# A run-time overflow test on the sums of exponentials, with a branch to a general path

## The chip, the core and the metric

The kernel runs on one core of one Trainium2 chip. The core has five engines with their own instruction streams: PE (matrix multiply into PSUM), DVE (vector), ACT (activation functions), POOL (general vector work) and SP (which here only issues transfers). They meet through semaphores. The time is device microseconds of one execution. The three timed runs of the kernel before took 146.16, 146.58 and 146.92 us, median 146.58. A separate execution was profiled; all views below are of it.

## The reference

One token block x of 2048 tokens by 512 channels goes through two branches, and a per-token gate mixes them:

```
qkv = x @ wqkv; q, k, v in 32 heads of 16
pq = q @ w_phi[h]; pk = k @ w_phi[h]
phi_q = concat(softmax(pq), softmax(-pq)); phi_k = concat(softmax(pk), softmax(-pk))
kv = sum_s phi_k[s] v[s]; z = sum_s phi_k[s]
a = ((phi_q @ kv) / (phi_q @ z + 1e-6)) @ wo
b = relu(x @ w1) @ w2
g = sigmoid((x * gate_w).sum(-1))
out = g * a + (1 - g) * b
```

All inputs and the output are bf16. The attention is linear: kv and z are sums over all tokens, so no query can be finished before the last key is in. The softmax runs over the 16 features of one head.

## The kernel before, in words

The tokens are cut into NT = 16 tiles of 128. The work is written down by hand as one list of operations per engine (`_Plan.op`, `_Plan.dma`); each entry names the events that it waits for, and `emit` (L45) turns the list of an engine into instructions, in exactly that order, with one counting semaphore per producer. An engine's list is therefore its queue: an operation waits behind everything in front of it.

Before the tile loop the kernel loads x, transposes it, computes the first chunk of h = relu(x @ w1) (`slab`, L549, `hunit`, L261) and folds w_phi into wqkv (`pre`, L303). Because a softmax does not change when a constant is taken off all its inputs, only 15 features per head are multiplied, each already reduced by feature 16; the 16th exponential is a constant 1 written once into EB (L579). No maximum is subtracted.

The attention stage handles one tile per step. `atile(m)` (L322) multiplies x by the folded weights into two PSUM banks, ACT takes exp of the plus and minus form into the buffer `EB[:, b]` (b = m mod 5; slots 0 and 1 for q, 2 and 3 for k). `kchain` (L383) sums the 16 features on DVE into the right half of `ZB[:, b]` (L392), takes the reciprocal (L394) and scales on POOL (L396). `qchain` (L402) sums q's features into the left half of ZB (L405), takes a reciprocal (L410), and POOL scales one half (L412, L414); SP then issues a DMA transpose to PHQ (L419). `kv(m)` (L439) adds phi_k transposed times v into banks 6 and 7, three tiles behind. Between these, PE is filled with pieces of h for later chunks (`mid`, L598). The last two tiles are done in halves.

After the last kv, `kvfin` (L454) moves kv and z to SBUF, and the final stage begins. `nd(m)` (L476) multiplies phi_q by kv and z on PE into banks 0 and 1 (even m) or 2 and 3 (odd m), DVE takes a reciprocal (`rd`, L486) and a product (`om`, L490) into one of three buffers OTM, and SP issues a transpose into OT (`to`, L496). `finB(m)` (L501) is h @ w2, 11 matmuls; `finA(m)` (L511) is OT @ wo, 4 matmuls, and ACT scales it by the gate (`ta`, L518). `comb(m)` (L523) adds both on DVE (`cb`, L527) into one of three buffers OSB and issues the output transfer (`out`, L532). `gate()` (L469) makes g and 1-g from exp. OTM and OSB lie in WQK, whose weights are no longer needed by then. The last tile's output is cut into 384 and 128 columns; the first part is sent by SP, the second by ACT, and SP waits for the `fin` semaphore (L674).

The order at the start of the final stage is nd(0), the last qchain, gate, finB(0), nd(1), finB(1), nd(2), nd(3), finA(0).

Of the kernel before, what the change touches and what calls it, by code (L numbers as in the profile page):

```python
# [5 lines left out]
ACT = mybir.ActivationFunctionType  # L6
ALU = mybir.AluOpType
# [6 lines left out]
class _Plan:  # L14


    def __init__(self, engines):
        self.ops = {e: [] for e in engines}
        self.count = {}
        self.events = {}  # L20
        self.first = {}

    def early(self, eng):
        self.first[eng] = len(self.ops[eng])

    def op(self, eng, fn, after=(), ev=None):
        if ev is not None:
            self.count[eng] = self.count.get(eng, 0) + 1
            self._set(ev, eng, self.count[eng])
        self.ops[eng].append((fn, tuple(after), eng if ev is not None else None, 1))  # L30
# [11 lines left out]
        assert ev not in self.events, ev  # L42
        self.events[ev] = (sem, value)

    def emit(self, name, eng, sems, block):  # L45
        seen = {}
        start = len(block)
        gate = next(i for i, ins in enumerate(block)
                    if ins.engine == eng.engine and ins.concise_opcode() == "EventSemaphore") if name in self.first else 0
        for k, (fn, after, sem, inc) in enumerate(self.ops[name]):  # L50
            if k == self.first.get(name):
                new = block[start:]
                del block[start:]
                block[gate:gate] = new
            need = {}
            for ev in after:
                s, v = self.events[ev]
                need[s] = max(need.get(s, 0), v)
            for s, v in need.items():
                if seen.get(s, 0) < v:  # L60
                    seen[s] = v
                    eng.wait_ge(sems[s], v)
            if fn is not None:
                ins = fn(eng)
                if sem is not None:
                    ins.then_inc(sems[sem], inc)


def bass_gated_mix__linear_kernel_hedgehog__dense_activation_relu__prompt_kernel(
# [17 lines left out]
    P = 128  # L87
# [13 lines left out]
    LAG = 3  # L101
    KU = KT - 1
    NR = DFF - KU * P

    with ExitStack() as es:
        E = es.enter_context
# [31 lines left out]
        OMG = E(nc.sbuf_tensor("OMG", [P, NT], FP32))  # L138
        RDEN = E(nc.sbuf_tensor("RDEN", [P, 2, H], FP32))
        TFA = E(nc.sbuf_tensor("TFA", [P, 2, D], BF16))  # L140
        PS = E(nc.psum_tensor("PS", [P, 8, 512], FP32))

        XS = OT[:, 0, :].rearrange("p (j d) -> p j d", j=4)
        WQKT = PHQ[:, :, S - 512:S]
        OTM = WQK[:, 0, 0:3 * D].rearrange("p (a b) -> p a b", a=3)
        OSB = WQK[:, 1, 0:3 * D].rearrange("p (a b) -> p a b", a=3)
        EPS = 8 * 512
        EBS = NB * 4 * 2 * D
        ones = bass.AP(tensor=ONE, offset=0, ap=[[1, P], [0, 512]])
# [172 lines left out]
        def atile(m, b0=0):  # L322
            b = m % NB
            first = xready(m // 4)
            order = [(dt, w) for dt in range(NDT) for w in range(2)]
            if m - 1 in split:
                order = [(dt, w) for w in (1, 0) for dt in range(NDT)]
            if m == 0:
                order = [(dt, w) for w in (0, 1) for dt in range(NDT)]
            for i, (dt, which) in enumerate(order):  # L330
                p.op("pe", lambda e, dt=dt, which=which: e.matmul(  # L331
                    PS[:, b0 + which, 0:DE], XT[:, dt, m * P:(m + 1) * P], WQK[:, which, dt * DE:(dt + 1) * DE],
                    start=(dt == 0), stop=(dt == NDT - 1)),
                    after=(first if i == 0 else []) + (free[b0 + which] if dt == 0 else [])
                    + ([f"pc{4 * which + dt}"] if m == 0 else []),
                    ev=(f"qk{m}" if i == 7 else None))
            src = PS[:, b0:b0 + 2, 0:DE].rearrange("p a (h f) -> p a h f", h=H)
            base = b * 8 * D
            busy = [f"tq{m - NB}", f"pk{m - NB}", f"pq{m - NB}"] if m >= NB else []

            def expo(s, w, ev):
                step = (4 * D, 2 * D)[s]
                off = base + s * (2 * D + 16)
                scale = (1.0, -1.0)[s]
                if w is None:
                    dst = bass.AP(tensor=EB, offset=off, ap=[[EBS, P], [step, 2], [32, H], [1, FE]])
                    s_ = src
                else:
                    dst = bass.AP(tensor=EB, offset=off + w * step, ap=[[EBS, P], [32, H], [1, FE]])
                    s_ = src[:, w, :, :]  # L350
                p.op("act", lambda e: e.activation(dst, s_, ACT.Exp, scale=scale),  # L351
                     after=[f"qk{m}"] + busy, ev=ev)
# [12 lines left out]
            qchain(m)  # L365

        def half(m, w, bank):
            b = m % NB
# [33 lines left out]
        def qchain(m):  # L402
# [17 lines left out]
                out=PHQ[:, :, m * P:(m + 1) * P], in_=EB[:, b, 0, :]),  # L420
                f"tq{b}", after=[f"pq{m}", f"cst{b}"] + (["pm7"] if m == 12 else []), ev=f"tq{m}")

        def vtile(m, eng="act", bank=2):
            b = m % VB
            for dt in range(NDT):
                p.op("pe", lambda e, dt=dt: e.matmul(  # L426
                    PS[:, bank, :], XT[:, dt, m * P:(m + 1) * P], WV[:, dt, :],
                    start=(dt == 0), stop=(dt == NDT - 1)),
                    after=((xready(m // 4) + ["wv"] + free[bank]) if dt == 0 else ()),
                    ev=(f"v{m}" if dt == NDT - 1 else None))  # L430
            dst, src = VS[:, b, :, 0:64], PS[:, bank, :].rearrange("p (g c) -> p g c", g=NG)
# [7 lines left out]
        def kv(m):  # L439
            b = m % NB  # L440
            vb = m % VB
            for g in range(NG):
                after = []
                if g == 0:
                    after = [f"pk{m}", f"cv{m}", f"one{vb}"]
                    if m == 0:
                        after += free[6] + free[7]
                p.op("pe", lambda e, g=g: e.matmul(  # L448
                    PS[:, 6 + g // 4, (g % 4) * GW:(g % 4) * GW + 65],
                    EB[:, b, 3, g * P:(g + 1) * P], VS[:, vb, g, 0:65],  # L450
                    start=(m == 0 and g % 4 == 0), stop=(m == NT - 1), skip_group_check=True),
                    after=after, ev=(f"kv{m}" if g == NG - 1 else None))
# [14 lines left out]
                free[6 + hf] = [f"kvz{hf}"]  # L467

        def gate():  # L469
            p.op("dve", lambda e: e.tensor_single_scalar(EG[:, :], EG[:, :], 1.0, ALU.add),  # L470
                 after=[f"eg{c}" for c in range(NCH)], ev="egp")
            p.op("dve", lambda e: e.reciprocal(GT[:, :], EG[:, :]), after=["egp"], ev="g")
            p.op("dve", lambda e: e.tensor_scalar(OMG[:, :], GT[:, :], -1.0, 1.0, ALU.mult, ALU.add),
                 after=["g"], ev="gt")
# [174 lines left out]
        nd(0)  # L649
        qchain(NT - 1)  # L650
        gate()
        finB(0, 4)
        nd(1)
        FB = (4, 5, 7)
        for m in range(NT):
            if m > 1 and m + 3 < NT:
                nd(m + 3)
            if m + 1 < NT - 1:
                finB(m + 1, FB[(m + 1) % 3])
            if m == 1:  # L660
                nd(m + 3)
            if m == 0:
                nd(2)
                nd(3)
            finA(m, (6, 2, 0)[max(m - NT + 3, 0)])
            if m < NT - 1:
                comb(m)
        m = NT - 1
        cuts = [slice(0, 384), slice(384, 512)]
        for i, cs in enumerate(cuts):  # L670
            finB(m, (4, 3)[i], cs, "ab"[i])
        for i, cs in enumerate(cuts):
            comb(m, cs, "ab"[i], ("sp", "act")[i])
        p.wait("sp", [f"out{NT - 1}b"])  # L674

        sems = {}
        for name in p.count:
            sems[name] = nc.alloc_semaphore(f"s_{name}")
        for name, eng in (("sp", nc.sync), ("act", nc.scalar), ("pe", nc.tensor), ("dve", nc.vector), ("pool", nc.gpsimd)):
            p.emit(name, eng, sems, nc.cur_bb.bb.instructions)  # L680


# [26 lines left out]
```

## Time and profile before

| Quantity | Value |
|---|---|
| Time of the profiled execution | 146.39 us |
| Its span (first to last own instruction) | 145.1 us |
| Outside the span | 1.29 us |
| Median of three timed runs | 146.58 us |
| PE busy | 142.5 us (98%) |
| DVE busy | 92.6 us (64%), 160 instructions |
| ACT busy | 73.2 us (50%) |
| POOL busy | 51.2 us (35%) |
| Granted PE clock | 1.00 |

The span is shorter than the time, since work at the start and end that is not the program's own lies outside it. The share of busy time of an engine is a mean over stages: the attention stage runs from about 22 to 87 us, the final stage from there to the end. In the timeline, neighbouring instructions of one line are merged into one row with a count. "SPq" and "ACTq" rows are transfers being issued, not their duration on the DMA engines.

### The profile page before, as it was taken

Reading aid. Unit: us, or ns where it says so; the run is one execution under the profiler, and the core shown is the slowest. Engines: PE = TensorE matmul, PEld = TensorE weight load, DVE = VectorE, ACT = ScalarE, POOL = GpSimd, SP = SyncE. Lnnn points to the kernel's source line nnn. Section 1 sums busy time; section 2 is a strip of 40 time slices with the busy share of each in tenths; the row PEclk is TensorE's granted clock in tenths of the full one; section 3 lists DMA queues with packets and bytes.
Section 4 is the critical chain, followed back from the end, with each engine's and each line's share of the span. In section 5 each row is a group of like instructions: output and inputs, shape, how many; then the busy total and the mean of one; then the engine's idle time right before and its main releaser. Section 6 shows DMA issues by size and latency. Waiting matters only on the chain.

```text
span 145.1 us, 2524 instructions
## 1 busy us (share of the span) xinstructions
PE 142.5 (98%) x973; PEld 73.0 (50%) x973; DVE 92.6 (64%) x160; ACT 73.2 (50%) x125; POOL 51.2 (35%) x59
## 2 busy tenths in 40 slices
PE   8999999999999999999999999999999999999994
PEld 3544754444545545655464545554444544445443
DVE  4338837988768678787887938664455555545342
ACT  5124579777788877877898861122111111111150
POOL 2000202998668886866889231200000000000000
DMA  5998997044308988332353513355232223222213
GB/s 143 296 275 163 263 163 144 5 104 108 75 10 200 317 116 226 72 72 49 66 72 73 108 38 75 79 104 135 70 86 72 72 72 77 72 72 75 72 45 106
DMA packets 46389, 16.12 MB, mean 111 GB/s; under 512 B 40392, under 2 KB 45992, under 8 KB 46376
## 3 DMA queue, kind: packets, MB, share of 16 engines
q1 hardware_dynamic: 46224, 15.92, 49.4%
q8 instruction: 8, 0.13, 0.4%
q10 hardware_dynamic: 152, 0.03, 0.1%
q14 instruction: 5, 0.04, 0.1%
HBM read 4.15 MB, written 2.10 MB: 43 GB/s over the span
## 4 chain that ended last, share of the span: by engine, by line
PE 96%; DMA 2%; DVE 1%; issue 0%
PE PS L504 26%; PE PS L264 19%; PE PS L331 16%; PE PS L426 10%; PE PS L513 10%; PE PS L551 4%; PE PS L480 3%; PE PS L448 3%; PE PS L371 2%; PE PS L276 2%; DMA W<-in_B_w_dram 2%; PE PS L309 1%; PE PS L543 1%; DVE WQK L527 1%; PE PS L216 0%
## 5 line engine op out<-in xcount | busy, mean ns | idle before, releaser
L504 PE MATMUL PS<-W,HT 128*128 128x512 bf16 (+2 forms) x187 | 40.6, 366 | 0.0
L396 POOL TENSOR_TENSOR EB<-EB,SC 128x1024 bf16<-128x1024 bf16 x15 | 28.9, 1928 | 17.2 <-DVE SC L394 17.2
L518 ACT ACTIVATE TFA<-PS,GT 128x512 bf16<-128x512 f32 x16 | 11.0, 687 | 42.6 <-PE PS L513 42.6
L351 ACT ACTIVATE EB<-PS 128x960 bf16<-128x960 f32 (+1 forms) x36 | 26.1, 797 | 11.8 <-PE PS L331 11.8
L264 PE MATMUL PS<-XT,W 128*128 128x512 bf16 x128 | 30.9, 379 | 0.0
L527 DVE SCALAR_TENSOR_TENSOR WQK<-PS,OMG,TFA 128x512 bf16<-128x512 f32 (+2 forms) x17 | 12.2, 719 | 23.6 <-ACT TFA L518 22.3
L504 PEld LDWEIGHTS PS<-W,HT 128*128 128x128 bf16 x187 | 17.0, 98 | 17.4
L392 DVE TENSOR_REDUCE ZB<-EB 128x64 f32<-128x1024 bf16 x15 | 18.2, 1212 | 11.7 <-ACT EB L351 11.5
L331 PE MATMUL PS<-WQK,XT 128*128 128x480 bf16 x112 | 24.8, 366 | 0.0
L250 ACT ACTIVATE HT<-PS 128x512 bf16<-128x512 f32 x35 | 20.6, 613 | 8.2 <-PE PS L551 5.8
L405 DVE TENSOR_REDUCE ZB<-EB 128x64 f32<-128x1024 bf16 x16 | 18.7, 1167 | 0.0
L264 PEld LDWEIGHTS PS<-XT,W 128*128 128x128 bf16 x128 | 12.0, 98 | 13.2
L414 POOL TENSOR_TENSOR EB<-EB,SC 128x512 bf16<-128x512 bf16 x16 | 16.9, 1056 | 1.2
L331 PEld LDWEIGHTS PS<-WQK,XT 128*128 128x128 bf16 x112 | 10.9, 98 | 11.8
L513 PE MATMUL PS<-WO,OT 128*128 128x512 bf16 x64 | 16.1, 379 | 0.0
L426 PE MATMUL PS<-WV,XT 128*128 128x512 bf16 x64 | 15.9, 378 | 0.0
L490 DVE TENSOR_TENSOR WQK<-PS,RDEN 128x512 bf16<-128x512 f32 x16 | 11.1, 691 | 0.6
L436 ACT ACTIVATE VS<-PS 128x512 bf16<-128x512 f32 x14 | 8.6, 612 | 3.1 <-PE PS L426 3.1
L513 PEld LDWEIGHTS PS<-WO,OT 128*128 128x128 bf16 x64 | 6.1, 98 | 7.1
L394 DVE RECIPROCAL SC<-ZB 128x64 f32<-128x64 f32 x16 | 8.8, 553 | 0.5
L486 DVE RECIPROCAL RDEN<-PS 128x32 f32<-128x32 f32 x16 | 5.6, 349 | 4.1 <-PE PS L480 4.1
L426 PEld LDWEIGHTS PS<-WV,XT 128*128 128x128 bf16 x64 | 5.4, 97 | 4.8
(64 smaller groups left out, 96.9 us busy)
## 6 DMA issues: line engine op xcount, KB each, us to landing
out_dram<-WQK SPq DMA_DIRECT2D x15, 128.0 KB, 1.7
W<-in_B_w_dram SPq DMA_DIRECT2D x2, 640.0 KB, 5.6
W<-in_B_w_dram SPq DMA_DIRECT2D x2, 256.0 KB, 3.2
WV<-in_A_wqkv_dram SPq DMA_DIRECT2D x1, 512.0 KB, 5.9
WO<-in_A_wo_dram SPq DMA_DIRECT2D x2, 256.0 KB, 3.9
W<-in_B_w_dram SPq DMA_DIRECT2D x1, 344.0 KB, 4.1
W<-in_B_w_dram SPq DMA_DIRECT2D x1, 264.0 KB, 4.8
OT<-in_A_x_dram SPq DMA_DIRECT2D x2, 128.0 KB, 2.3
```

The lines of the kernel that those rows point to most:

```text
L250: p.op("act", lambda e: e.activation(dst, src, ACT.Relu), after=[f"h{c}_{kt}"], ev=ev)
L264: p.op("pe", lambda e, t=t: e.matmul(PS[:, bank, :], W1[:, t, kt * P:(kt + 1) * P], XT[:, t, c * 512:(c + 1) * 512], start=(t == 0), stop= ...
L331: p.op("pe", lambda e, dt=dt, which=which: e.matmul(PS[:, b0 + which, 0:DE], XT[:, dt, m * P:(m + 1) * P], WQK[:, which, dt * DE:(dt + 1) ...
L351: p.op("act", lambda e: e.activation(dst, s_, ACT.Exp, scale=scale), after=[f"qk{m}"] + busy, ev=ev)
L392: p.op("dve", lambda e: e.tensor_reduce(zk, ek, AX.X, ALU.add), after=[emk, f"cst{b}"], ev=f"zk{m}")
L396: p.op("pool" if m < NT - 1 else "dve", lambda e: e.tensor_tensor(EB[:, b, 3, :].rearrange("p (g f) -> p g f", f=DH), EB[:, b, 2, :].rearr ...
L405: p.op("dve", lambda e: e.tensor_reduce(ZB[:, b, 0:64].rearrange("p (h s) -> p h s", s=2), bass.AP(tensor=EB, offset=base, ap=[[EBS, P], [ ...
L414: p.op("pool", lambda e: e.tensor_tensor(EB[:, b, 0, :].rearrange("p (h s f) -> p h s f", h=H, s=2)[:, :, 1, :], EB[:, b, 1, :].rearrange( ...
L426: p.op("pe", lambda e, dt=dt: e.matmul(PS[:, bank, :], XT[:, dt, m * P:(m + 1) * P], WV[:, dt, :], start=(dt == 0), stop=(dt == NDT - 1)), ...
L504: p.op("pe", lambda e, kt=kt: e.matmul(PS[:, bank, 0:n], HT[:, kt, m * P:(m + 1) * P], W2[:, kt, cs], start=(kt == 0), stop=(kt == KT - 1) ...
L513: p.op("pe", lambda e, t=t: e.matmul(PS[:, bank, :], OT[:, t, m * P:(m + 1) * P], WO[:, t, :], start=(t == 0), stop=(t == NDT - 1)), after ...
L527: p.op("dve", lambda e: e.scalar_tensor_tensor(out=OSB[:, ob, cs], in0=PS[:, bank, 0:n], scalar=OMG[:, m:m + 1], in1=TFA[:, m % 2, cs], op ...
```

## The change

The change keeps the fast path and adds a test of whether its exponentials were too large, and a second, general path behind a branch. It has these parts.

Test. `top(m)`, one DVE reduction per tile, takes the largest of the 128 sums in each row of ZB into a column of ZM. `flag()` reduces the 16 columns to one (ZT) and SP issues a transfer that turns the column of 128 floats into one row (ZR). `flag2()`, issued on DVE at step m = 8 of the final loop, reduces that row to one number and compares it with 1e18, giving the integer FLAG.

Reading it. At step m = 13 SP, DVE and ACT are told to wait for `flag`; behind this point `emit` puts, on each of the four engines SP, ACT, PE and DVE, one instruction that loads FLAG into a register, before the rest of that engine's list. PE's load stands behind its last matmul.

Branch. At the end each of the four engines compares its register with zero and branches. Where the flag is 0 it jumps over a body to the end, where SP waits for `fin`. The body, executed only if the flag is set, is the `slow` plan: `_Serial` runs one operation at a time with a single semaphore, and recomputes attention with a maximum (and minimum) subtracted in `guarded(m)`, then the whole final stage. It holds 688 matmuls, 340 DVE operations, 160 ACT operations and 48 transfers.

What makes room for it. WQK must survive for the body, so OTM and OSB move from WQK to EB (buffers 1 and 2, slots 2 and 3). `gate()` clamps exp at 1e30 in the same instruction that adds 1.

```diff
+    def here(self, eng):
+        self.mark[eng] = len(self.ops[eng])
...
-    def emit(self, name, eng, sems, block):
-        seen = {}
+    def emit(self, name, eng, sems, block, part):
+        seen = self.seen[name]
+        cut = self.mark.get(name, len(self.ops[name]))
...
         for k, (fn, after, sem, inc) in enumerate(self.ops[name]):
+            if (k >= cut) != bool(part):
+                continue
...
+class _Serial:
...
+    def emit(self, engines, sem, total=0):
+        for name, fn, inc in self.ops:
+            eng = engines[name]
+            if total:
+                eng.wait_ge(sem, total)
+            fn(eng).then_inc(sem, inc)
+            total += inc
+        engines["sp"].wait_ge(sem, total)
...
-        OTM = WQK[:, 0, 0:3 * D].rearrange("p (a b) -> p a b", a=3)
-        OSB = WQK[:, 1, 0:3 * D].rearrange("p (a b) -> p a b", a=3)
+        OTM = EB[:, 1, 2:4, :].rearrange("p a (b c) -> p (a b) c", c=D)
+        OSB = EB[:, 2, 2:4, :].rearrange("p a (b c) -> p (a b) c", c=D)
...
             kchain(m, emk)
             qchain(m)
+            top(m)
...
+        def top(m):
+            b = m % NB
+            p.op("dve", lambda e: e.tensor_reduce(ZM[:, m:m + 1], ZB[:, b, :], AX.X, ALU.max),
+                 after=[f"zk{m}", f"zq{m}"], ev=f"top{m}")
+
+        def flag():
+            p.op("dve", lambda e: e.tensor_reduce(ZT[:, :], ZM[:, :], AX.X, ALU.max),
+                 after=[f"top{NT - 1}"], ev="zt")
+            p.dma("sp", lambda e: e.dma_start(out=ZR[0:1, :], in_=ZT[:, 0:1]), "zr", after=["zt"], ev="zr")
+
+        def flag2():
+            p.op("dve", lambda e: e.tensor_reduce(ZX[:, :], ZR[:, :], AX.X, ALU.max), after=["zr"], ev="zx")
+            p.op("dve", lambda e: e.tensor_single_scalar(FLAG[:, :], ZX[:, :], LIMIT, ALU.is_gt),
+                 after=["zx"], ev="flag")
...
-            p.op("dve", lambda e: e.tensor_single_scalar(EG[:, :], EG[:, :], 1.0, ALU.add),
+            p.op("dve", lambda e: e.tensor_scalar(EG[:, :], EG[:, :], 1e30, 1.0, ALU.min, ALU.add),
...
         qchain(NT - 1)
         gate()
+        top(NT - 2)
+        top(NT - 1)
+        flag()
         finB(0, 4)
         nd(1)
...
             if m < NT - 1:
                 comb(m)
+            if m == 8:
+                flag2()
+            if m == NT - 3:
+                for eng in ("sp", "dve", "act"):
+                    p.wait(eng, ["flag"])
+                    p.here(eng)
...
-        p.wait("sp", [f"out{NT - 1}b"])
+        p.wait("pe", ["flag"])
+        fast, p = p, _Serial()
+        def guarded(m):
...
+        for m in range(NT):
+            vtile(m)
+            guarded(m)
+            kv(m, 0)
+        kvfin()
+        for m in range(NT):
+            nd(m)
+            finB(m, 4)
+            finA(m, 5)
+            comb(m)
+        slow, p = p, fast
...
+        for name, eng in engines.items():
+            p.emit(name, eng, sems, nc.cur_bb.bb.instructions, 0)
+        over = nc.values_load(FLAG[0:1, 0:1], engines=[engines[n].engine for n in ("sp", "act", "pe", "dve")],
+                              min_val=0, max_val=1, skip_runtime_bounds_check_because="it is a comparison's result")
+        for name, eng in engines.items():
+            p.emit(name, eng, sems, nc.cur_bb.bb.instructions, 1)
+        again = nc.alloc_semaphore("s_again")
+        with nc.If(over > 0):
+            nc.sync.wait_ge(sems["fin"], p.count["fin"])
+            nc.sync.sem_inc(again, 1)
+            for name in ("act", "pe", "dve"):
+                engines[name].wait_ge(again, 1)
+            slow.emit(engines, again, 1)
+        nc.sync.wait_ge(sems["fin"], p.count["fin"])
```

More of the change, by code (lines that the diff above doesn't have):

```diff
@@ L21, in __init__ @@
         self.first = {}
+        self.mark = {}
+        self.seen = {e: {} for e in engines}
     def early(self, eng):
         self.first[eng] = len(self.ops[eng])
+    def here(self, eng):
+        self.mark[eng] = len(self.ops[eng])
     def op(self, eng, fn, after=(), ev=None):
@@ L43, in _set @@
         self.events[ev] = (sem, value)
-    def emit(self, name, eng, sems, block):
-        seen = {}
+    def emit(self, name, eng, sems, block, part):
+        seen = self.seen[name]
+        cut = self.mark.get(name, len(self.ops[name]))
         start = len(block)
-        gate = next(i for i, ins in enumerate(block)
-                    if ins.engine == eng.engine and ins.concise_opcode() == "EventSemaphore") if name in self.first else 0
+        gate = next(i for i, ins in enumerate(block) if ins.engine == eng.engine
+                    and ins.concise_opcode() == "EventSemaphore") if name in self.first and not part else 0
         for k, (fn, after, sem, inc) in enumerate(self.ops[name]):
+            if (k >= cut) != bool(part):
+                continue
             if k == self.first.get(name):
@@ L66, in emit, with __init__, op, dma @@
                     ins.then_inc(sems[sem], inc)
+class _Serial:
+    def __init__(self):
+        self.ops = []
+    def op(self, eng, fn, after=(), ev=None):
+        self.ops.append((eng, fn, 1))
+    def dma(self, eng, fn, sem, after=(), ev=None):
+        self.ops.append(("sp", fn, 16))
+    def emit(self, engines, sem, total=0):
[6 more added lines that the diff above has]
+        engines["sp"].wait_ge(sem, total)
 def bass_gated_mix__linear_kernel_hedgehog__dense_activation_relu__prompt_kernel(
@@ L103, in bass_gated_mix__linear_kernel_hedgehog__dense_activation_relu__prompt_kernel @@
     NR = DFF - KU * P
+    LIMIT = 1e18
     with ExitStack() as es:
@@ L140, in bass_gated_mix__linear_kernel_hedgehog__dense_activation_relu__prompt_kernel @@
         TFA = E(nc.sbuf_tensor("TFA", [P, 2, D], BF16))
+        ZM = E(nc.sbuf_tensor("ZM", [P, NT], FP32))
+        ZT = E(nc.sbuf_tensor("ZT", [P, 1], FP32))
+        ZR = E(nc.sbuf_tensor("ZR", [1, P], FP32))
+        ZX = E(nc.sbuf_tensor("ZX", [1, 1], FP32))
+        FLAG = E(nc.sbuf_tensor("FLAG", [1, 1], I32))
         PS = E(nc.psum_tensor("PS", [P, 8, 512], FP32))
@@ L437, in vtile, with kv @@
             free[bank] = [f"cv{m}"]
-        def kv(m):
-            b = m % NB
+        def kv(m, b=None):
+            b = m % NB if b is None else b
             vb = m % VB
@@ L673, in bass_gated_mix__linear_kernel_hedgehog__dense_activation_relu__prompt_kernel @@
             comb(m, cs, "ab"[i], ("sp", "act")[i])
-        p.wait("sp", [f"out{NT - 1}b"])
+        p.wait("pe", ["flag"])
+        fast, p = p, _Serial()
+        def guarded(m):
+            for w, bank in ((0, 0), (1, 1)):
+                for dt in range(NDT):
+                    p.op("pe", lambda e, w=w, bank=bank, dt=dt: e.matmul(
+                        PS[:, bank, 0:DE], XT[:, dt, m * P:(m + 1) * P], WQK[:, w, dt * DE:(dt + 1) * DE],
+                        start=(dt == 0), stop=(dt == NDT - 1)))
+                d = PS[:, bank, 0:DE].rearrange("p (h f) -> p h f", h=H)
+                for s in range(2):
+                    lim = SC[:, s, 0:H]
+                    dif = ZB[:, :, :].rearrange("p a b -> p (a b)")[:, 0:DE].rearrange("p (h f) -> p h f", h=H)
+                    raw = EB[:, 0, w, :].rearrange("p (h s f) -> p h s f", h=H, s=2)[:, :, s, :]
+                    al, sg = ((ALU.max, 1.0), (ALU.min, -1.0))[s]
+                    p.op("dve", lambda e, d=d, lim=lim, al=al: e.tensor_reduce(lim, d, AX.X, al))
+                    p.op("dve", lambda e, lim=lim, al=al: e.tensor_single_scalar(lim, lim, 0.0, al))
+                    p.op("dve", lambda e, d=d, lim=lim, dif=dif: e.tensor_tensor(
+                        dif, d, lim.unsqueeze(2).to_broadcast([P, H, FE]), ALU.subtract))
+                    p.op("act", lambda e, raw=raw, dif=dif, sg=sg: e.activation(
+                        raw[:, :, 0:FE], dif, ACT.Exp, scale=sg))
+                    p.op("act", lambda e, raw=raw, lim=lim, sg=sg: e.activation(
+                        raw[:, :, FE:DH], lim.unsqueeze(2), ACT.Exp, scale=-sg))
+                raw = EB[:, 0, w, :].rearrange("p (g f) -> p g f", f=DH)
+                phi = EB[:, 0, 2 + w, :].rearrange("p (g f) -> p g f", f=DH)
+                p.op("dve", lambda e, raw=raw: e.tensor_reduce(SC[:, 2, 0:2 * H], raw, AX.X, ALU.add))
+                p.op("dve", lambda e: e.reciprocal(SC[:, 3, 0:2 * H], SC[:, 2, 0:2 * H]))
+                p.op("dve", lambda e, raw=raw, phi=phi: e.tensor_tensor(
+                    phi, raw, SC[:, 3, 0:2 * H].unsqueeze(2).to_broadcast([P, 2 * H, DH]), ALU.mult))
+            p.dma("sp", lambda e: e.dma_start_transpose(out=PHQ[:, :, m * P:(m + 1) * P], in_=EB[:, 0, 2, :]), "")
@@ L676, in bass_gated_mix__linear_kernel_hedgehog__dense_activation_relu__prompt_kernel @@
+        for m in range(NT):
[9 more added lines that the diff above has]
+        slow, p = p, fast
+        engines = {"sp": nc.sync, "act": nc.scalar, "pe": nc.tensor, "dve": nc.vector, "pool": nc.gpsimd}
         sems = {}
@@ L678, in bass_gated_mix__linear_kernel_hedgehog__dense_activation_relu__prompt_kernel @@
             sems[name] = nc.alloc_semaphore(f"s_{name}")
-        for name, eng in (("sp", nc.sync), ("act", nc.scalar), ("pe", nc.tensor), ("dve", nc.vector), ("pool", nc.gpsimd)):
-            p.emit(name, eng, sems, nc.cur_bb.bb.instructions)
+        for name, eng in engines.items():
[12 more added lines that the diff above has]
+        nc.sync.wait_ge(sems["fin"], p.count["fin"])
 _INS = ['A_x', 'A_wqkv', 'A_w_phi', 'A_wo', 'B_x', 'B_w1', 'B_w2', 'gate_w']
```

## The prediction

> **What bounds the kernel now.** I read the page's busy shares first, then the chain of work that ended last, then the timeline at three places that the change touches: the attention stage, its seam with the final stage, and the last 10 us.
>
> ```profile
> PE 142.5 (98%) x973; PEld 73.0 (50%) x973; DVE 92.6 (64%) x160; ACT 73.2 (50%) x125; POOL 51.2 (35%) x59
> ...
> PE 96%; DMA 2%; DVE 1%; issue 0%
> ```
>
> PE is the bound: from 3.76 us to 142.5 us the chain is matmul after matmul, and the waits of PE sum to 0.6 us, all at the start. So an operation added on DVE, ACT or SP costs nothing unless it makes a matmul late, or lies behind the last matmul. The change leaves PE's order of matmuls as it was. What DVE has spare in the attention stage is in the groups of instructions by shape (busy us, mean ns, idle before):
>
> ```profile
> L405 DVE TENSOR_REDUCE ZB<-EB 128x64 f32<-128x1024 bf16 x16 | 18.7, 1167 | 0.0
> L392 DVE TENSOR_REDUCE ZB<-EB 128x64 f32<-128x1024 bf16 x15 | 18.2, 1212 | 11.7 <-ACT EB L351 11.5 <-ACT EB L378 0.2
> ...
> L389 DVE TENSOR_REDUCE ZB<-EB 128x32 f32<-128x512 bf16 x2 | 1.3, 680 | 0.5 <-ACT EB L378 0.5
> ```
>
> DVE waits 11.7 us for ACT over 15 tiles. The seam, by the timeline (start, duration):
>
> ```profile
> 90.17 0.25 DVE L472 RECIPROCAL GT<-EG 128x16 f32<-128x16 f32 x1
> ...
> 90.45 0.17 DVE L473 TENSOR_SCALAR OMG<-GT 128x16 f32<-128x16 f32 x1
> ...
> 90.53 0.35 DVE L486 RECIPROCAL RDEN<-PS 128x32 f32<-128x32 f32 x1
> 90.92 0.69 DVE L490 TENSOR_TENSOR WQK<-PS,RDEN 128x512 bf16<-128x512 f32 x1
> 91.60 1.23 SPq L419 DMA_TRANSPOSE PHQ<-EB  x1
> ...
> 92.31 0.67 PE L480 MATMUL PS<-KVNZ,PHQ 128*128 128x68 bf16 x16
> 92.76 0.36 DVE L486 RECIPROCAL RDEN<-PS 128x32 f32<-128x32 f32 x1 [1.15 <-PE PS L480]
> ...
> 92.87 3.89 SPq L496 DMA_TRANSPOSE OT<-WQK  x3
> ```
>
> The reader sees the new work's place (behind L473, before rd1 and om1 at 90.53) and 1.15 us of idle DVE behind om1. And the end, where everything behind 142.5 us is exposed:
>
> ```profile
> 139.02 0.69 ACT L518 ACTIVATE TFA<-PS,GT 128x512 bf16<-128x512 f32 x1 [2.55 <-PE PS L513]
> 139.79 1.61 DVE L527 SCALAR_TENSOR_TENSOR WQK<-PS,OMG,TFA 128x512 bf16<-128x512 f32 x2 [2.54 <-ACT TFA L518]
> ...
> 142.53 0.96 DVE L527 SCALAR_TENSOR_TENSOR WQK<-PS,OMG,TFA 128x384 bf16<-128x384 f32 x2 [1.13 <-PE PS L504]
> 143.53 0.38 ACTq L532 DMA_DIRECT2D out_dram<-WQK  x1
> ```
>
> **The change part by part.**
>
> Tile maxima. No row has a 128 to 1 reduction; the two reduction shapes fix a line: (1212 - 680) / 512 = 1.04 ns per element and 148 ns fixed, so 128 elements take 0.28 us. Ends: 0.11 us (L470, 128x16) and 0.68 us (L389). 14 of them lie in the attention stage, 14 x 0.28 = 3.9 us against 11.7 us of idle. The tightest places are tiles 0 to 2, where DVE runs without a gap from 22.52 to 32.05 us (then idle 0.51): 3 x 0.28 = 0.84, so tile 3 is 0.3 us late and tile 4 (1.19 idle) takes it back; and tiles 11 to 14, idle 0.32, 0.20 and 0.52, where one maximum each leaves at most 0.1 us of lateness. What is late next is phi_k: POOL ends tile 14's at 80.7 (78.77 + 1.93) and PE's kv for it starts at 83.10, 2.4 us later. No matmul waits; cost 0. At the 0.68 end each tile would slip 0.3 to 0.4 us, some 3 us by tile 14, and about 0.6 us would reach PE; that is in the range.
>
> Gate clamp: L470 becomes a two-operation form, like L473 (0.17 against 0.11 us), +0.06 on DVE.
>
> Seam. Two maxima and the reduction of 16 columns (0.17 by L473's width): 0.56 + 0.17 + 0.06 = 0.8 us between L473 and rd1. om1 ends at 91.61 + 0.8 = 92.4 instead. Behind it waits nd(3), which reuses om1's banks: of the 16 matmuls that start at 92.31 the second eight start 0.26 later, at 92.57. 0.2 us remain: 0. If a maximum cost 0.68, om1 would be 1.6 us late and nd(3) 0.6 us late. On SP the new transfer stands behind tile 15's transpose (issued 91.60 to 92.83) and in front of to1: with an issue of 0.34 to 0.58 us (L532) to1 starts at about 93.3 instead of 92.87, lands 2.5 us later at 95.8, and its reader finA(1) starts at 96.31. Also 0; to2, to3 and out0 are later by the same half microsecond, with 2 us and more to spare.
>
> The comparison at m = 8: two DVE operations of 0.11 to 0.28 us, in the 1.75 us that DVE waits for ACT in every step; the row that they read was sent 25 us earlier. 0.
>
> Waits and loads on SP, DVE and ACT at m = 13. The flag is set 15 us before, so the waits are free. The trace shows no register load; its nearest rows are a semaphore instruction (0.02 us) and the smallest transfer (1.5 us from issue to landing). Behind it are, on ACT, ta14 (idle 2.55 before it), on DVE cb14 (idle 2.54), on SP out14, which can't go before cb14 ends. 1.5 us fit: 0. The cover is the wait for finA(14); without it the price would be up to 1.5 us.
>
> OTM and OSB in EB: same shapes, same engines, and their last readers there are the kv products of tiles 11 and 12. 0.
>
> PE's load. It stands behind the last matmul: 142.5 us plus 0 to 1.5. Against a full price speaks that PE's last semaphore instruction is at 136.6 us, so its sequencer is done with waits 5.9 us before its matmuls are. I take 1.5, since the load reads SBUF and is nearest to a small transfer.
>
> The branch. With the flag 0 every one of four engines jumps over its body. The trace has no taken branch. What it does have is instruction transfers:
>
> ```profile
> q8 instruction: 8, 0.13, 0.4%
> ...
> q14 instruction: 5, 0.04, 0.1%
> ```
>
> The instructions are fed in pieces of 16 KB (0.13 MB / 8) and 8 KB while the program runs. 0.4% of 16 x 145.1 us over 8 is 1.2 us for a large piece, 0.1% over 5 is 0.5 us for a small one. A jump over 688 matmuls with their weight loads lands beyond what straight running has brought, so I price one feed: latency of the smallest transfer, 1.5, plus its piece: 2.7 us on PE, 2.0 on DVE and ACT. Ends: 0.05 us (a semaphore instruction of PE) and two feeds one behind the other, 5.4. SP's body is 48 transfers; taken as 0.
>
> [...]
>
> Sum of the ends. SP's last wait ends at 145.1 as before. ACT: 143.53 + 0.38 + 2.0 = 145.9. DVE: 143.49 + 2.0 = 145.5. PE: 142.5 + 1.5 + 2.7 = 146.7. PE is last, 1.6 us behind the old end. Against the profiled execution, 146.39 + 1.6 = 148.0; the median of the runs stands 0.19 higher, so 148.2.
>
> **The rivals.** (1) All hidden: the load and jump of PE run while its matmuls are still queued, and ACT's target is already there. For it: the 136.6 us above. Against: ACT's jump cannot start before 143.9, which leaves 1.2 us. The time stays 146.6; with the half microsecond of a seam stall 147.2. (2) A dearer jump: two feeds and the load on PE, 142.5 + 1.5 + 5.4 = 149.4, 4.3 behind the old end: 150.9. For it: four engines refill at once. Against: the packets are short and the DMA engines about a quarter busy. (3) Faster: reading output and transpose data from EB instead of WQK shortens the last transfer. Only its landing counts, 1.5 us behind 143.53; it decides if 0.8 of it goes, 145.8. Nothing in the trace speaks for it. (4) The flag comes out 1 and the body runs: 688 matmuls in single file at 0.37 us are 250 us more; the inputs are scaled by 0.05, so sums near 1e18 are excluded, under 1%.
>
> **How the numbers follow.** 0.5% (0.73 us) is about what a measurement can tell from no change. Chances: forecast 0.52 (own range 147.3 to 149.5), rival 1 0.27, rival 2 0.16, faster 0.04, body 0.01. So faster 0.04, same 0.27, slower 0.69. The range has to take in rival 1 and the dear end of rival 2: 146.4 to 150.9.
>
> **What would show it.** PE's busy time and the order of matmuls unchanged, no new PE wait near 92.5 us; maxima near 0.28 us; the last out transfer landing near 145.1; and additions behind 142.5: PE's register load and branch, extra instruction packets. Wrong it would be if PE gets a wait in the attention stage, if the last output itself is late (a load of over 2.5 us on DVE or ACT), or if the end of the program is not kept by the jumping engines at all.

## The result and the profile after

| | Before | Changed |
|---|---|---|
| Median of six executions | 146.43 us | 148.94 us |
| Lowest and highest | 146.16 to 147.13 | 148.09 to 149.44 |
| Profiled execution | 146.39 us | 148.17 us |
| Its span | 145.1 us | 145.5 us |
| Its time outside the span | 1.3 us | 2.7 us |

The change makes the kernel slower by 1.55% (ratio 1.0155, 95% interval 1.0111 to 1.0199). One execution in the experiments (of e3) took 856.68 us; its cause is open and it enters no comparison.

The table already says where to look: 1.4 of the profiled execution's 1.8 us lie behind or before the span. The page's first lines of the changed kernel show the added work and no new bound:

```profile
PE 141.3 (97%) x956; PEld 72.8 (50%) x973; DVE 95.6 (66%) x179; ACT 73.2 (50%) x125; POOL 51.3 (35%) x59
...
q8 instruction: 9, 0.15, 0.4%
q14 instruction: 7, 0.06, 0.2%
```

DVE has 19 instructions and 3.0 us more. PE shows 17 matmuls fewer, which are missing records: its weight loads are 973 as before. There are three more instruction packets in the span than the 8 and 5 of before.

The chain that ended last, of before (start, duration), at the first matmuls on the weights of h, at the first full slab, at nd(0) and at the end:

```profile
3.76 1.61 PE PS L543 x8
5.37 6.04 PE PS L551 x28
...
87.22 0.26 PE PS L480 x8
...
138.12 2.59 PE PS L513 x12
140.71 1.80 PE PS L504 x11
142.51 0.03 issue
142.53 0.96 DVE WQK L527 x2
```

The same of the changed kernel:

```profile
3.63 1.37 PE PS L595 x8
5.00 6.04 PE PS L603 x28
...
86.84 0.26 PE PS L532 x8
...
137.74 2.59 PE PS L565 x12
140.33 1.80 PE PS L556 x11
142.13 0.02 issue
142.16 0.97 DVE EB L579 x2
```

Every piece starts 0.37 or 0.38 us earlier, from the first slab to the last DVE operation. In this execution the first weights were used 0.13 us earlier and the eight matmuls on them took 0.24 us less; from there on no matmul moved against another. So nothing was lost in 137 us of matmuls, and the profiled execution would have been 0.37 us faster had the end not changed. The end did: by the views of the lines of the loads (L785) and of the branches (L796), where a "q" behind the engine marks its sequencer and the three numbers are ns:

```profile
L785 ACTq TENSOR_LOAD <-FLAG x1: 472/472/472, 138.6 to 138.6; - x1
L785 DVEq TENSOR_LOAD <-FLAG x1: 542/542/542, 139.4 to 139.4; - x1
L785 SPq TENSOR_LOAD <-FLAG x1: 550/550/550, 140.6 to 140.6; - x1
L785 PEldq TENSOR_LOAD <-FLAG x1: 546/546/546, 140.8 to 140.8; - x1
...
L796 PEldq COMPARE_BRANCH  x1: 3362/3362/3362, 141.5 to 141.5; - x1
L796 DVEq COMPARE_BRANCH  x1: 72/72/72, 142.8 to 142.8; - x1
L796 SPq COMPARE_BRANCH  x1: 45/45/45, 143.2 to 143.2; - x1
L796 ACTq COMPARE_BRANCH  x1: 54/54/54, 143.6 to 143.6; - x1
L796 SPq EVENT_SEMAPHORE  x1: 17/17/17, 145.5 to 145.5; - x1
```

A load takes 0.47 to 0.55 us. PE's branch takes 3.4 us, but begins at 141.5, while matmuls still run (until 142.13). The others' branches are over in 45 to 72 ns. A wait of theirs for what lies behind the jump is in no record; outside the span are 2.7 us, against 1.3 before. And the last wait of SP ends at 145.5 although the last transfer was issued 0.4 us earlier than before. The transfers in the last microseconds, by queue, of the changed kernel between 141 and 148 us (packets, MB, share of 16 engines), and the landings of the two parts of the last output (the time from issue to arrival) from a view of the output tensor:

```profile
q1 hardware_dynamic: 432, 0.36, 15.1%
q10 hardware_dynamic: 144, 0.03, 2.1%
q14 instruction: 4, 0.03, 1.9%
q8 instruction: 2, 0.03, 1.7%
...
DMA to landing us min/median/max: 1.8/2.0/2.3
```

The same two views of before:

```profile
q1 hardware_dynamic: 432, 0.36, 15.6%
q10 hardware_dynamic: 144, 0.03, 2.2%
...
DMA to landing us min/median/max: 1.5/1.6/1.6
```

The window held the same 432 and 144 packets and no instruction packet. Now six instruction packets are in it, three of them behind the end of the span, and the last transfer takes 0.8 us longer to land. The sum for this execution: 1.4 outside, 0.8 landing, less 0.4 of earlier start: 1.8.

The medians differ by 2.5 us: 1.4 outside, and 1.15 in the span. The landing is 0.8 of that; the other 0.35 is of the size by which starts scatter and is not explained further. In the profile of e5, the changed kernel again at 148.98 us, the first slab took 6.45 us instead of 6.04, while from nd(0) to the last DVE operations it is 55.3 us as in the two profiles above.

### The profile page after: what moved, and what is told of

The parts are those of the page before. It is cut to its first block, busy times and chain, and to the rows that moved or that the text cites. A ratio compares the mean times of both kernels' runs of the same rounds, so it can differ in the third digit from the quotient of the medians.

```text
span 145.5 us, 2535 instructions
## 1 busy us (share of the span) xinstructions
PE 141.3 (97%) x956; PEld 72.8 (50%) x973; DVE 95.6 (66%) x179; ACT 73.2 (50%) x125; POOL 51.3 (35%) x59
## 4 chain that ended last, share of the span: by engine, by line
PE 95%; DMA 2%; issue 1%; DVE 1%
PE PS L556 26%; PE PS L300 19%; PE PS L367 16%; PE PS L565 9%; PE PS L478 9%; PE PS L603 4%; PE PS L532 3%; PE PS L500 3%; PE PS L408 2%; PE PS L312 2%; DMA W<-in_B_w_dram 2%; PE PS L345 1%; PE PS L595 1%; DVE EB L579 1%; PE PS L252 0%
## 5 line engine op out<-in xcount | busy, mean ns | idle before, releaser
L556 PE MATMUL PS<-W,HT 128*128 128x512 bf16 (+2 forms) x182 | 40.0, 366 | 0.3
L300 PE MATMUL PS<-XT,W 128*128 128x512 bf16 x122 | 29.7, 379 | 0.3
L579 DVE SCALAR_TENSOR_TENSOR EB<-PS,OMG,TFA 128x512 bf16<-128x512 f32 (+2 forms) x17 | 12.2, 719 | 23.2 <-ACT TFA L570 22.0
L478 PE MATMUL PS<-WV,XT 128*128 128x512 bf16 x60 | 15.4, 378 | 0.2
L542 DVE TENSOR_TENSOR EB<-PS,RDEN 128x512 bf16<-128x512 f32 x16 | 11.1, 691 | 0.6
```

Of the source, the lines that this page charges most:

```text
L300: p.op("pe", lambda e, t=t: e.matmul(PS[:, bank, :], W1[:, t, kt * P:(kt + 1) * P], XT[:, t, c * 512:(c + 1) * 512], start=(t == 0), stop= ...
L478: p.op("pe", lambda e, dt=dt: e.matmul(PS[:, bank, :], XT[:, dt, m * P:(m + 1) * P], WV[:, dt, :], start=(dt == 0), stop=(dt == NDT - 1)), ...
L556: p.op("pe", lambda e, kt=kt: e.matmul(PS[:, bank, 0:n], HT[:, kt, m * P:(m + 1) * P], W2[:, kt, cs], start=(kt == 0), stop=(kt == KT - 1) ...
L579: p.op("dve", lambda e: e.scalar_tensor_tensor(out=OSB[:, ob, cs], in0=PS[:, bank, 0:n], scalar=OMG[:, m:m + 1], in1=TFA[:, m % 2, cs], op ...
```

## The experiments

Four explanations were to be told apart. The feed theory: an engine that jumps over a long body has to have the instructions behind it fetched, and the program ends when the last of them has them. Against it: the added DVE work, the transfer and the loads cost the time; a branch costs by itself, whatever its distance; and, within the feed theory, which engine is last (the prediction said PE). Each experiment edits the changed kernel; short diffs follow. In the executions with the flag at 0 the body is never run, so a body that is cut leaves the executed work as it is.

All results in one table. Time and span are medians of the executions of a run, "outside" is the median of time less span, the ratio is to the kernel before on the same chip. Medians of spans carry up to 0.4 us of the start's scatter; "outside" does not: it was 1.23 to 1.34 us in the 17 executions before. Where the text gives a landing or the time of a packet or a branch, it is that of the profiled execution of the run.

| Run | Time | Span | Outside | Ratio (95%) |
|---|---|---|---|---|
| before (17 executions) | 146.41 | 145.1 | 1.30 | 1 |
| changed, first run | 148.94 | 146.25 | 2.72 | 1.0155 (1.0111 to 1.0199) |
| e5 changed again | 148.89 | 146.2 | 2.69 | 1.0157 (1.0132 to 1.0182) |
| e1 short body | 146.67 | 145.35 | 1.31 | 1.0012 (0.9991 to 1.0034) |
| e2 ACT's body alone | 147.95 | 145.1 | 2.83 | 1.0118 (1.0082 to 1.0154) |
| e3 DVE's body alone | 148.34 | 145.9 | 2.50 | 1.0130 (1.0093 to 1.0166) |
| e4 PE's body alone | 147.09 | 145.2 | 1.68 | 1.0052 (1.0023 to 1.0081) |
| e10 without DVE's body | 148.37 | 145.75 | 2.66 | 1.0125 (1.0091 to 1.0160) |
| e11 without PE's body | 148.57 | 145.95 | 2.53 | 1.0145 (1.0112 to 1.0179) |
| e7 output by SP | 148.60 | 146.2 | 2.40 | 1.0159 (1.0134 to 1.0184) |
| e8 constant flag | 148.47 | 146.3 | 2.22 | 1.0162 (1.0131 to 1.0192) |
| e6 early branches | 147.32 | 145.4 | 1.68 | 1.0070 (1.0051 to 1.0089) |
| e9 hints | 148.40 | 146.0 | 2.35 | 1.0126 (1.0097 to 1.0155) |
| e12 early branches and hint | 147.16 | 145.8 | 1.30 | 1.0041 (1.0021 to 1.0061) |

### Is it the jump? e1, e8, e5

```diff
         slow, p = p, fast
+        slow.ops = []
```

> The body of the branch is left with its waits alone (the general path is left out); the maxima, the flag, the four register loads and the four branches stay. Feed theory (the time is lost because the jumping engines must have the instructions behind the body fetched): the target now lies a few instructions on, no engine fetches, the span goes back to about 145.1 us plus or minus 0.3 and the time to 146.4 to 146.8 us. Rival A (the test and the loads themselves cost the time): 148.2 us or more, as in the changed kernel. Rival B (the branch instruction costs by itself, whatever its distance): 147.5 us or more.

```diff
-            top(m)
...
-        top(NT - 2)
-        top(NT - 1)
-        flag()
...
             if m == 8:
-                flag2()
+                p.op("dve", lambda e: e.memset(FLAG[:, :], 0), ev="flag")
```

> The maxima, their reductions and the small transfer are left out (the test itself is not computed: the flag is a constant 0 written at m = 8); loads, branches and the full body stay. Feed theory: no gain, 148.2 to 149.4 us. Rival (the 19 added DVE operations or the extra transfer at the seam make something late): 146.4 to 147.8 us.

The changed kernel without any edit was run again beside it:

> The changed kernel once more, to see how its extra time splits into the span and what lies behind it. Feed theory: span 145.1 to 146.6 us, 2.5 to 2.8 us outside it against 1.3 of the kernel before; time 148.1 to 149.4 us. If the time is lost inside the span (test, loads): outside stays at 1.3.

e1 has all maxima, loads and branches, and nothing left to jump over: 146.67 us, no difference from before that can be told. Outside is back at 1.31, and so are the landings and PE's branch (views of the branch line and of the output tensor of e1):

```profile
L797 PEldq COMPARE_BRANCH  x1: 231/231/231, 142.2 to 142.2; - x1
...
DMA to landing us min/median/max: 1.5/1.6/1.7
```

The same branch instruction took 0.23 us on PE with a near target (e1) and 3.36 with a far one (the changed kernel). e8 is the counterpart: without the maxima, their reduction and the transfer, but with the full body, it is as slow as the changed kernel. Its loss splits otherwise, with 2.22 us outside and a landing of 2.6; why is open. So the test and the loads cost nothing that can be measured; the jump over the body costs all of it. Both rivals fell. e5 splits its extra time as the first run did.

### Which engine? e2, e3, e4, e10, e11

```diff
         slow, p = p, fast
+        slow.ops = [o for o in slow.ops if o[0] == "act"]     ("dve" in e3, "pe" in e4)
```

> Of the body only ACT's 160 instructions are kept; SP, PE and DVE jump a short way (the general path is left incomplete). Feed theory with ACT as the last engine: ACT branches at about 143.6 us, fetches, and is back at about 146.4, so 147.7 to 148.3 us, and one or two small instruction packets near 144.5. Rival (PE's 3.4 us branch sets the time): PE doesn't fetch here, so 146.4 to 146.8 us.

> Of the body only DVE's 340 instructions are kept (the general path is left incomplete). Feed theory: DVE branches at about 142.8 us and is back at about 145.8, 0.7 us behind the last output, so 146.9 to 147.5 us. If PE or ACT alone sets the time: 146.4 to 146.8 us.

> Of the body only PE's 688 matmuls are kept (the general path is left incomplete). Feed theory with ACT as the last engine: PE's branch starts while matmuls are still queued (141.5 us), takes 3.4 us and ends at about 144.9, before the last output has landed, so 146.4 to 146.9 us. Rival (PE's branch sets the time): 147.7 us or more.

e2 came out as expected, 147.95. e4 is 0.2 us over its expectation (147.09 against 146.4 to 146.9): PE is hardly the engine that counts most, though alone it costs 0.7 us, clear of noise. e3 missed by 0.8 us: DVE's jump is dearer than I had it, and also delays the output. Landing and instruction packets between 141 and 148 us, e3 first (KB, then us to landing):

```profile
q14 instruction: 2, 0.02, 0.6%
...
out_dram<-EB ACTq DMA_DIRECT2D x1, 32.0 KB, 2.7
```

and e2, with as many packets in the window:

```profile
q14 instruction: 2, 0.02, 0.7%
...
out_dram<-EB ACTq DMA_DIRECT2D x1, 32.0 KB, 1.5
```

The last output, both parts together, is 288 packets on its queues. By the packets' own times, in e2 all are moved by 144.4 us and the first instruction packet begins at 144.55. In e3 the first begins at 144.54 and 18 packets of the output are moved only between 144.8 and 145.6 us, all others by 144.5. In the changed kernel it is again 18, between 144.5 and 144.85. 18 is one sixteenth of 288, the share of one of 16 DMA engines. That this is the engine which also brings the instructions fits the times: in the five runs changed, e3, e5, e8 and e11, the first of the 18 begins within 0.01 us of the end of an 8 KB instruction packet (144.46, 144.84, 145.17, 145.11 and 144.55 us). But the records do not name the engine that a packet took, and in e3 the others of the output had ended by 144.53, just before that instruction packet began, so what held the 18 until then is open.

What a jump costs can be worked out from the three profiled executions, if the 1.3 us outside the span before are the same everywhere. From the start of the branch to the end less 1.3: ACT 147.55 - 1.3 - 143.64 = 2.6 us, DVE 148.60 - 1.3 - 142.99 = 4.3, PE 147.18 - 1.3 - 141.48 = 4.4, of which the branch record itself is 3.7. PE's is an upper bound: the record ends at 145.16, when SP's last wait ends too, so the last output may have set that end.

```diff
         slow, p = p, fast
+        slow.ops = [o for o in slow.ops if o[0] != "dve"]     ("pe" in e11)
```

> The changed kernel without DVE's part of the body (the general path is left incomplete); ACT's, PE's and SP's stay. If DVE's fetch is the last to end in the changed kernel: ACT's is next, 147.4 to 148.2 us, as in the run with ACT's body alone, and the landing of the last output goes back to about 1.6 us. If ACT's fetch is the last: 148.2 us or more, no gain.

> The changed kernel without PE's part of the body (the general path is left incomplete); ACT's, DVE's and SP's stay. If DVE's fetch is the last to end: no gain, 148.2 to 149.0 us. If PE, which the prediction had as the last, sets the time: 147.5 us or less.

e11: no clear gain without PE's body, as expected if PE is not last. e10 fits neither of its cases whole: 148.37 lies in the range for ACT as the last and is not clearly under the changed kernel's time, but the landing went back to 1.8 us, as in the other case. Outside stays at 2.66, near that with ACT's body alone. So there is no single last engine: DVE branches 0.8 us before ACT and needs some 1.7 us longer, and by these sums the two come back within a microsecond of each other. With DVE's part away ACT's is left (e10); the next run takes ACT's out of the way.

### Moving the jumps: e7, e6

```diff
-            comb(m, cs, "ab"[i], ("sp", "act")[i])
+            comb(m, cs, "ab"[i], "sp")
```

> The changed kernel with the second part of the last output issued by SP, so that ACT has nothing to wait for behind its last scaling and branches 3 us earlier, at about 140.6. Feed theory: ACT's fetch is hidden, DVE's (branch at 142.8) is left, and the output goes 0.3 us later: 148.2 to 148.8 us, as with DVE's body alone. If ACT's fetch alone sets the changed kernel's time: 146.6 to 147.3 us.

ACT's branch moved from 143.6 to 140.3 us, and the time stayed, as expected (148.60, 2.40 outside): DVE's jump holds it. PE's body is in it too, but e4 and e11 put PE's share low. This agrees with e3.

```diff
-            if m == NT - 3:
+            if m == NT - 4:
                 for eng in ("sp", "dve", "act"):
...
-        for name, eng in engines.items():
-            p.emit(name, eng, sems, nc.cur_bb.bb.instructions, 1)
...
         with nc.If(over > 0):
+            for name, eng in engines.items():
+                p.emit(name, eng, sems, nc.cur_bb.bb.instructions, 1)
             nc.sync.wait_ge(sems["fin"], p.count["fin"])
...
             slow.emit(engines, again, 1)
...
+        with nc.Else():
+            for name, eng in engines.items():
+                p.emit(name, eng, sems, nc.cur_bb.bb.instructions, 1)
```

> The whole change, but SP, ACT and DVE load the flag and branch one step earlier (m = 12), while PE still has 6 us of matmuls; what they have left to do stands in both arms of the branch. PE still branches behind its last matmul. Feed theory: ACT's and DVE's fetches of some 3 us run beside PE's matmuls, only PE's own is left, as in the run with PE's body alone: 146.6 to 147.2 us. Rival (a jump costs its time wherever it stands, since it makes ta and cb late): 148.0 us or more.

ACT and DVE now branch at 136.1 and 136.9 us, while PE has its last 6 us of matmuls; what they still have to do stands behind the jump. More than half of the loss is gone: 147.32, a tenth over the expected range and with it on the theory's side, not the rival's. DVE waits 2.80 us instead of 2.54 before its next operation and has caught up by the last matmul. What is left, 1.68 us outside, is as in e4 with PE's body alone.

### Asking for the instructions early: e9, e12

```diff
         for m in range(NT):
...
+            if m == 4:
+                for name in ("act", "pe", "dve"):
+                    p.op(name, lambda e, name=name: hints.__setitem__(name, e.mark_branch_hint_location()))
...
-        with nc.If(over > 0):
+        for name in ("sp", "act", "pe", "dve"):
+            jump = engines[name].br_cond(over > 0, "again_true", "again_end")
+            if name in hints:
+                jump.branch_hint(hints[name])
...
```

> The whole change with one hint instruction more on each of ACT, PE and DVE, at step m = 4, some 25 us before the end, which names the branch to come, so that the instructions behind the body are brought early; nothing else is altered. Feed theory: no packet of instructions is left between the branches and the end, PE's branch takes 0.2 us as in the run with the short body instead of 3.4, the last output lands 1.5 us after its issue again and 1.3 to 1.4 us lie outside the span: 146.3 to 146.9 us. Rival (the branch or the loads cost by themselves, or the hint names the wrong side): 148.2 to 149.4 us.

In this edit each of ACT, PE and DVE has one hint instruction, which the program ties to that engine's branch. The three ran at 105.2 (PE), 107.8 (ACT) and 108.5 us (DVE), some 36 us before their branches and not 25. The hint worked on PE and not as a whole (view of the branch line in e9):

```profile
L795 PEldq COMPARE_BRANCH  x1: 632/632/632, 141.8 to 141.8; - x1
L795 DVEq COMPARE_BRANCH  x1: 90/90/90, 143.1 to 143.1; - x1
L795 SPq COMPARE_BRANCH  x1: 45/45/45, 143.5 to 143.5; - x1
L795 ACTq COMPARE_BRANCH  x1: 68/68/68, 143.9 to 143.9; - x1
```

PE's branch fell from 3.4 to 0.6 us, but the time only to 148.40 and outside to 2.35. Small packets still start at 144.3, 144.9 and 147.3, the first two, by their distance from the branches, perhaps one each for DVE and ACT. The theory's expectation failed, and the time lies in the rival's range. The rival's reasons don't hold for PE, whose branch fell, and e1 spoke against a price of the branch by itself; whether the hints of ACT and DVE came too early, or hints don't help there, was not tried further.

```diff
+            if m == 4:
+                p.op("pe", lambda e: hints.__setitem__("pe", e.mark_branch_hint_location()))
...
+        four = ("sp", "act", "pe", "dve")
+        for name in four:
+            jump = engines[name].br_cond(over > 0, "again_true", "again_false")
+            if name in hints:
+                jump.branch_hint(hints[name])
...
```

(with the two arms of e6 as `again_true` and `again_false`)

> The early branches of e6 (SP, ACT and DVE at m = 12, the rest of their work in both arms) together with the hint for PE's branch of e9 at m = 4; the whole change is kept. Feed theory: ACT's and DVE's fetches lie beside PE's matmuls, PE's branch takes some 0.6 us, so what was left in e6 (0.3 to 0.6 us outside the span, or a late landing) shrinks: 146.3 to 147.0 us, below e6's 147.32. If it is the packets of instructions as such, not the waiting for them, that cost the rest: 147.0 to 147.5 us, as e6.

The time outside the span is back at 1.30, that of the kernel before, in the median of twelve executions: no engine is seen to end late any more, though the whole body is still in the program (PE's branch takes 0.88 us here). The time is 147.16, not the 146.4 that this alone would give, and above the range that I gave the theory, in that of the rival. The last output still lands late, with one instruction packet left in the last microseconds, PE's by its queue and size, since the window of e4, with PE's body alone, has only such packets of 16 KB on q8 (queues between 141 and 148 us, and the view of the output tensor):

```profile
q8 instruction: 1, 0.02, 0.9%
...
DMA to landing us min/median/max: 1.7/1.9/2.1
```

So the loss has two parts, which e12 separates: time outside the span, by the theory that of engines that wait for instructions (gone here, 1.30 us), and a late last output (left, 2.1 us to landing). That instruction packets make it late rests on times. In e6, e10, e4 and e12, where PE's 16 KB packet is the only one of instructions in flight while the last transfer moves, it ended 0.32, 0.55, 0.62 and 0.89 us after the issue of the last transfer, and that landed after 1.6, 1.8, 1.9 and 2.1 us: the later the packet, the later the output.

e12 has the lowest median of the versions with the whole test, 0.41% behind the kernel before; its interval overlaps that of e6. None is faster than the kernel before.

## Why the prediction was right, and where it was not

Direction, size and place were right: slower, 148.2 forecast and 148.94 measured, and the cost behind the last matmul. The working of the sum was right in kind and wrong in which term counted.

- Maxima: 0.28 us forecast, 0.23 measured. DVE's idle time before the sums of k fell from 11.7 to 9.6 us, and no matmul moved. The groups of the changed kernel by shape:

```profile
L429 DVE TENSOR_REDUCE ZB<-EB 128x64 f32<-128x1024 bf16 x15 | 18.3, 1217 | 9.6 <-ACT EB L387 9.6
...
L462 DVE TENSOR_REDUCE ZM<-ZB 128x1 f32<-128x128 f32 x16 | 3.7, 234 | 0.0
```

- Seam: the work between the gate and rd1 took 0.6 us (forecast 0.8), and ate half of the slack that was named (idle of 0.56 left of 1.15). The transfer's issue took 0.60 us and put the next transpose back by as much; its reader did not wait. The timeline of the changed kernel:

```profile
90.16 0.47 DVE L462 TENSOR_REDUCE ZM<-ZB 128x1 f32<-128x128 f32 x2
...
90.67 0.17 DVE L466 TENSOR_REDUCE ZT<-ZM 128x1 f32<-128x16 f32 x1
90.75 0.35 DVE L538 RECIPROCAL RDEN<-PS 128x32 f32<-128x32 f32 x1
...
92.39 0.36 DVE L538 RECIPROCAL RDEN<-PS 128x32 f32<-128x32 f32 x1 [0.56 <-PE PS L532]
92.50 0.60 SPq L468 DMA_DIRECT2D ZR<-ZT  x1
```

- Loads at m = 13: free, as forecast, but not for the reason given. I took the idle 2.54 us before the DVE row at 139.79 for the gap behind cb13; the three finA of tiles 13 to 15 run back to back, so cb13 itself is the first operation of that row and the loads have no gap. The row of ACT was misread alike: the idle 2.55 us are before ta13. The loads are free because here a sequencer loads while its engine still works: DVE's load runs at 139.44 to 139.98 beside cb13 (139.42 to 140.17).
- PE's load: this step failed. It was put behind the last matmul with a full 1.5 us; it took 0.55 and began at 140.8, 1.3 us before the last matmul ended (142.13). So PE's branch began at 141.5 and not at 144.0; for PE this is what rival 1 said. The row that spoke against the price, PE's last semaphore instruction at 136.6, was the better guide.
- The branch: that a jump over the body costs time was right, the sizes per engine were not. I priced ACT and DVE at 2.0 us and PE at 2.7; from the runs they are 2.6, 4.3 and, for PE, 3.4 to 4.4. With PE's earlier start this turns the order round: PE, forecast as last, cost 0.7 us alone (e4) and nothing clear beside the others (e11), while ACT and DVE cost 1.5 and 1.9 alone (e2, e3).
- A term was missing: the last output was taken to land as before. It landed 0.8 us later. The prediction had named a late last output as a sign of being wrong, but by way of a slow load, which it was not.
- The two errors nearly cancelled. PE's load and jump were 1.6 of the 1.6 us forecast; in their place stand 1.4 outside the span by ACT and DVE and 0.8 by the landing. That the forecast came within 0.7 us of the median is in part luck.
- SP's jump, taken as 0, is 0.05 us in its record; no run tries it alone.

The trace of before has no branch instruction. That a far jump waits for one feed, and the prices of 2.7 and 2.0 us for it, were my estimate from the instruction packets and the smallest transfer there. e1 against the changed kernel bears out that distance counts: PE's branch took 0.23 us near and 3.36 far, and between 141 and 148 us there are no instruction packets in e1 and six in the changed kernel. The branch records of SP, ACT and DVE are 45, 54 and 72 ns in both, so they do not show the cost of a far jump.

## What to carry to other kernels

A rare path behind a branch was not free here, though it wasn't run: ACT, DVE and PE each lost time by jumping over their part of the body, 0.7 to 1.9 us one by one, and ACT and DVE lost none outside the span where they had microseconds of slack after the jump (e12: 1.30 us outside, as before). So let the engines branch while the bound engine still has queued work and put the rest of the fast path behind the jump, keep the last instructions of the program near the branch, and count the time outside the span, since the wait behind a jump may be recorded nowhere else: ACT's and DVE's branches are 54 and 72 ns in e1 and in the changed kernel, with 1.31 and 2.72 us outside. The 3.0 us of work added on DVE, which waits for ACT, made no matmul late here, as the idle rows said, with half of the slack at the seam used up.

## What was not expected

- A far jump of DVE (340 instructions) costs about 4.3 us, one of ACT (160) about 2.6. In both, two packets of 8 KB follow, of 0.3 to 0.4 us each in e2 and e3. ACT's first starts 0.9 us behind its branch in e2, DVE's 1.55 us in e3, while the last output is being moved; the rest of the difference is open.
- By the times of the packets, fetched instructions may have delayed the last output: with 8 to 16 KB of them among the packets of the last output, its 32 KB part landed after up to 2.7 us (e3) instead of 1.5.
- A register load from SBUF took 0.47 to 0.55 us on the four engines, and on DVE the sequencer did it beside cb13 (139.44 to 139.98 within 139.42 to 140.17).
- The page of the second run of the changed kernel shows a mean PE clock of 0.999. Up to 136 us its granted clock is 1.00 and in the last 10 us 0.99, and its matmuls keep the distances of before from nd(0) on, so the clock explains nothing of the difference.
